# Second token step of a 2-D Fourier filter and its inverse with real and imaginary parts on the partitions, and the middle of the kernel in written order

## The chip, the cores and the metric

The kernel runs on one core of one Trainium2 chip. The metric is the device time of one execution in microseconds (us), as the median of several runs. The engines are named as in the profile: PE (TensorE, with PEld for its weight loads), DVE (VectorE), ACT (ScalarE), POOL (GpSimd) and SP (SyncE, whose queue issues almost all DMAs).

## The reference

Two branches over the same input `x` (1 x 2048 x 1024) are mixed by a gate that is one number per token. Branch A filters `x` by a real two-dimensional Fourier transform, a complex product with a weight W of 2048 x 513, and the inverse. Branch B is a diagonal state-space model of 1024 complex states that runs over the 2048 tokens.

```
g = sigmoid(sum(x * gate_w, -1))
a = irfft2(rfft2(x) * (w_r + 1j*w_i))                      # branch A
h[t] = Lam_bar * h[t-1] + x[t] @ B_bar.T                    # branch B
b = 2 * real(h @ C.T) + x * Dskip
out = g * a + (1 - g) * b
```

All tensors are bf16 in and out.

## The kernel before

**Branch B** works in 16 *units*: 8 chunks `c` of 256 tokens, each in two halves `q` of the states. In `unit` (L203), PE makes the real and then the imaginary part in 32 products of 256 columns each (`psu`, L209; the two parts are called the two halves of a unit here), ACT copies each to a buffer `h` (L211), and DVE does the rest: two products and joins that turn the phases back, two scans (L223), a small carry to the next chunk, and the products and joins that turn them on. 6 buffers `h` stand in turn. From a chunk's two units come two *tiles* of 128 tokens: `c_gemm` (L456) makes `ps_y` in two halves of 16 products of 512 columns and 4 of 128 (Dskip).

**Branch A** is one generator, `gfnet` (L239). 2048 tokens are split as 128 x 16, so that the transform over tokens takes two steps with a turn through DRAM between them. *Step one* (16 times): `fd` transforms over the 1024 features (`ps_fd`, 8 products), and `ps_s1` over 128 tokens with tables T3 (4 products); the result A1 goes to `turn1_scratch`. *Step two* (`s2w`, 16 times): `Bb` comes back with 128 rows that hold 16 blocks of 8; real and imaginary part stand side by side in the free dimension, so `ps_s2` takes 4 products of 512 columns (L354 to L357), the complex product with W 4 instructions of DVE (L361 to L365). The *first inverse step*, `ps_is1` (L375 to L378), takes 4 products with T3, ACT evicts it to C1 and copies a corrected column (L381), and C1 goes to `turn2_scratch`. The *second inverse step* (L387 on) loads it as `Cq` (in the buffer `raw`) and makes `ps_is2` in 8 products of 256 columns; ACT writes ZT. The inverse over the features is `spectral` (`ps_id`, L485), 8 products for each tile.

Column 0 and column 512 are packed into one complex column. `fixup` (L283) unpacks them: the column goes through DRAM (`Acol`, `Bcol`), PE and DVE do a short chain of small steps up to `Qb`, and 64 one-column products (`cps`) make the corrected column of C1.

**Tiles.** 4 *early* tiles are multiplied out before ZT exists and wait in DRAM as `y_scratch` (fp32, eviction `ye`); 4 `late_tile` calls at the end add them. The other 12 are `own_tile`: the spectral part goes into the same PSUM tile by a product with `ident`.

**Order.** The code is traced in one order and a scheduler then sorts each engine's instructions by priority and readiness of their operands; `pull(budget)` (L434) says how much of `gfnet` is traced between two units, by credits such as the 1.73 of `yield 1.73`. PSUM has two pools of two tiles each: `psA` (branch A and own tiles) and `psU` (units, early tiles, `spectral`). Every wait of an engine holds what stands behind it.

Of the kernel before, what the change touches and what calls it, by code (L numbers as in the profile page):

```python
# [19 lines left out]
S = 2048  # L20
D = 1024
# [5 lines left out]
NEARLY = 4  # L27
# [8 lines left out]
def _host_consts():  # L36
# [12 lines left out]
    for cls in range(2):  # L49
# [18 lines left out]
    Kc, Ks = delta * np.cos(angK), delta * np.sin(angK)  # L68
    J = np.zeros((P, P))
# [9 lines left out]
        R12=b16(np.stack([np.concatenate([Kc, Ks], 1), np.concatenate([-Ks, Kc], 1)], 1)),  # L79
# [5 lines left out]
def kernel(  # L85
# [26 lines left out]
    cR12 = nc.inline_tensor(hc["R12"], name="c_R12").ap()  # L112
    cJP = nc.inline_tensor(hc["JP"], name="c_JP").ap()
    Wr_v = A_w_r.rearrange("(p b) k -> p b k", b=16)
    Wi_v = A_w_i.rearrange("(p b) k -> p b k", b=16)
# [85 lines left out]

    def unit(c, q):
        sh = [P, 2, 4, TC]  # L203
        u = halloc(sh, BF16)
        for ri in range(2):
            psu = psU.tile([P, 4, TC], FP32, name="psu", tag="psu")
            for j in range(4):
                for d8 in range(8):
                    nc.tensor.matmul(psu[:, j, :], lhsT=BT[4 * q + j][:, ri, d8, :],  # L209
                                     rhs=xT[:, d8, TC * c:TC * (c + 1)], start=(d8 == 0), stop=(d8 == 7))  # L210
            nc.scalar.copy(out=u[:, ri], in_=psu)  # L211
        js = slice(4 * q, 4 * q + 4)
        bc = lambda i: tab[:, i:i + 1, js, :].to_broadcast(sh)
        su = up.tile(sh, BF16, name="su")
        nc.vector.tensor_mul(out=su, in0=u[:, ::-1], in1=bc(1))  # L215
        nc.vector.tensor_mul(out=u, in0=u, in1=bc(0))  # L216
        nc.vector.tensor_add(out=u[:, 0], in0=u[:, 0], in1=su[:, 0])
        nc.vector.tensor_sub(out=u[:, 1], in0=su[:, 1], in1=u[:, 1])
        if c:
            nc.vector.tensor_add(out=u[:, :, :, 0], in0=u[:, :, :, 0], in1=carry[:, :, js])  # L220
        for ri in range(2):
            seg = u[:, ri].rearrange("p j t -> p (j t)")
            nc.vector.tensor_tensor_scan(out=seg, data0=rz[:, js].rearrange("p j t -> p (j t)"), data1=seg,  # L223
                                         initial=0.0, op0=ALU.mult, op1=ALU.add)
        if c + 1 < NCH:
            gl = u[:, :, :, TC - 1]
            nc.vector.tensor_mul(out=ck[:, 0, :, js], in0=gl, in1=cTC[:, js].unsqueeze(1).to_broadcast([P, 2, 4]))
            nc.vector.tensor_mul(out=ck[:, 1, :, js], in0=gl[:, ::-1], in1=sTC2[:, :, js])
            nc.vector.tensor_add(out=carry[:, :, js], in0=ck[:, 0, :, js], in1=ck[:, 1, :, js])
        sg = up.tile(sh, BF16, name="sg", tag="su")  # L230
        nc.vector.tensor_mul(out=sg, in0=u[:, ::-1], in1=bc(3))  # L231
        nc.vector.tensor_mul(out=u, in0=u, in1=bc(2))  # L232
        nc.vector.tensor_add(out=u[:, 0], in0=u[:, 0], in1=sg[:, 0])
        nc.vector.tensor_sub(out=u[:, 1], in0=u[:, 1], in1=sg[:, 1])
        hs[c, q] = u
# [4 lines left out]
    def gfnet():  # L240
        T3_sb, R12_sb, G_sb = fft["T3"], fft["R12"], fft["G"]
# [14 lines left out]
        for j in range(16):  # L256
# [14 lines left out]
            yield 2.6  # L271
# [6 lines left out]
        gt, wp, JP_sb = fft["gt"], fft["wp"], fft["JP"]  # L278
        Kc_sb, Ks_sb, Kns_sb = fft["K3"][:, 0], fft["K3"][:, 1], fft["K3"][:, 2]
        Wc = fft["Wc"]  # L280

        def fixup():
            zps = psA.tile([P, 2, 16], FP32, name="zps", tag="ps")  # L283
            nc.tensor.matmul(zps[:, 0, :], lhsT=Kc_sb, rhs=Bcol[:, :, 0], start=True, stop=False)
            nc.tensor.matmul(zps[:, 0, :], lhsT=Ks_sb, rhs=Bcol[:, :, 1], start=False, stop=True)
            nc.tensor.matmul(zps[:, 1, :], lhsT=Kc_sb, rhs=Bcol[:, :, 1], start=True, stop=False)
            nc.tensor.matmul(zps[:, 1, :], lhsT=Kns_sb, rhs=Bcol[:, :, 0], start=False, stop=True)
            Zp = fx.tile([P, 16, 2], BF16, name="Zp")
            nc.vector.tensor_copy(out=Zp, in_=zps.rearrange("p c b -> p b c"))
            Zp_f = fx.tile([P, 16, 2], FP32, name="Zp_f"); nc.vector.tensor_copy(out=Zp_f, in_=Zp)  # L290

            def reverse_m(src_bf, ncol, name):
                rps = psA.tile([P, 16, ncol], FP32, name=name + "_ps", tag="ps")
                for b in range(16):
                    if b == 0:
                        nc.tensor.matmul(rps[:, 0, :], lhsT=JP_sb[:, 1, :], rhs=src_bf[:, 0, :], start=True, stop=True)
                    else:
                        nc.tensor.matmul(rps[:, b, :], lhsT=JP_sb[:, 0, :], rhs=src_bf[:, 16 - b, :], start=True, stop=True)
                dst = fx.tile([P, 16, ncol], FP32, name=name)
                nc.vector.tensor_copy(out=dst, in_=rps)  # L300
                return dst

            Wc_f = fx.tile([P, 16, 4], FP32, name="Wc_f"); nc.vector.tensor_copy(out=Wc_f, in_=Wc)
            Wrev = reverse_m(Wc, 4, "Wrev")
            Wh = fx.tile([P, 16, 4], FP32, name="Wh")
            nc.vector.tensor_add(out=Wh[:, :, 0:4:2], in0=Wc_f[:, :, 0:4:2], in1=Wrev[:, :, 0:4:2])
            nc.vector.tensor_sub(out=Wh[:, :, 1:4:2], in0=Wc_f[:, :, 1:4:2], in1=Wrev[:, :, 1:4:2])
            alpha = fx.tile([P, 16, 2], FP32, name="alpha")
            nc.vector.tensor_add(out=alpha, in0=Wh[:, :, 0:2], in1=Wh[:, :, 2:4])
            nc.vector.tensor_scalar_mul(out=alpha, in0=alpha, scalar1=0.25)  # L310
            beta = fx.tile([P, 16, 2], FP32, name="beta")
            nc.vector.tensor_sub(out=beta, in0=Wh[:, :, 0:2], in1=Wh[:, :, 2:4])
            nc.vector.tensor_scalar_mul(out=beta, in0=beta, scalar1=0.25)
            Zr = reverse_m(Zp, 2, "Zrev")
            Q = fx.tile([P, 16, 2], FP32, name="Q")
            q1 = fx.tile([P, 16], FP32, name="q1")
            q2 = fx.tile([P, 16], FP32, name="q2")
            a_re, a_im, b_re, b_im = alpha[:, :, 0], alpha[:, :, 1], beta[:, :, 0], beta[:, :, 1]
            z_re, z_im, zr_re, zr_im = Zp_f[:, :, 0], Zp_f[:, :, 1], Zr[:, :, 0], Zr[:, :, 1]
            nc.vector.tensor_mul(out=q1, in0=a_re, in1=z_re)  # L320
# [26 lines left out]
        def s2w(b):  # L347
# [18 lines left out]
            return X3  # L366

        X3s = [s2w(0), s2w(1)]
        Ccol = fixup()
        for b in range(16):  # L370
            X3 = X3s.pop(0)
            if b + 2 < 16:
# [344 lines left out]
```

## Time and profile before

| | us |
|---|---|
| median of three runs | 396.24 (394.67 to 396.53) |
| the profiled execution | 396.38 |
| its span, first to last instruction | 394.6 |
| PE busy, by the page | 363.6 |
| DVE busy | 294.2 |
| ACT busy | 183.0 |

The span is what the trace shows, and 1.8 us of the execution lie around it. The busy time of PE is modelled (matmuls overlap), so it says where PE had something under way, not how much it got done. In three stretches the kernel reads as follows: up to 98 us `x` is loaded and turned, and step one runs; from 98 to 203 us come the column correction, step two, both inverse steps and parts of seven units and two tiles; from 203 us on, the remaining units, tiles and `spectral`.

### The profile page before, as it was taken

The page shows a single profiled execution, that of the slowest core. Times are in us where ns is not written, and L with a number is a line of the kernel's source. Part 1 is how long each engine was busy: PE and PEld are TensorE (multiplying, and loading weights), DVE is VectorE, ACT ScalarE, POOL GpSimd, SP SyncE. Part 2 cuts the span into 40 slices and gives each one's busy share as a digit, 9 for nine tenths or more (in the row PEclk, how much of TensorE's full clock was granted, in tenths as well). Part 3 has the DMA queues.
Part 4 walks back from the last instruction along what each step waited for, and adds up shares of the span by engine and source line. Part 5 has one row for each costly group of instructions (what it writes and reads, how often), then busy time and mean ns, then how long its engine had stood idle before and what let it go on. Part 6 is the DMA issues. An engine that isn't in the chain of part 4 may idle for free.

```text
span 394.6 us, 6556 instructions
## 1 busy us (share of the span) xinstructions
PE 363.6 (92%) x2625; PEld 239.6 (61%) x2625; DVE 294.2 (75%) x467; ACT 183.0 (46%) x234; POOL 28.8 (7%) x68
## 2 busy tenths in 40 slices
PE   4959998999899799898999999999999999999995
PEld 3836555557665444446777577586685775755552
DVE  2793679186989989896029789889898898897343
ACT  2649898664331288684962232142232231424331
POOL 6600000252300000000000000000000000000000
PEclk9979999999989789999999999999999999999999
DMA  7999921798580269857931010000000000001443
GB/s 205 345 179 241 191 110 55 186 202 184 141 236 8 86 197 318 278 191 193 269 98 55 1 55 28 0 28 27 2 28 0 29 27 2 27 28 27 135 130 110
DMA packets 58078, 45.85 MB, mean 116 GB/s; under 512 B 38720, under 2 KB 43200, under 8 KB 57792
## 3 DMA queue, kind: packets, MB, share of 16 engines
q1 hardware_dynamic: 57616, 45.41, 41.7%
q0 software_dynamic: 352, 0.02, 0.7%
q8 instruction: 20, 0.33, 0.3%
q14 instruction: 10, 0.08, 0.1%
q10 hardware_dynamic: 80, 0.01, 0.0%
HBM read 22.35 MB, written 14.69 MB: 94 GB/s over the span
## 4 chain that ended last, share of the span: by engine, by line
PE 61%; DVE 13%; DMA 11%; ACT 7%; SPq 3%; issue 3%; POOLq 1%; POOL 0%; ACTq 0%; DVEq 0%
PE ps_y L462 23%; PE psu L209 21%; PE ps_fd L249 5%; ACT X L252 3%; DMA Bb<-turn_scratch 3%; DMA raw<-turn_scratch 3%; DMA BT<-in_A_x_dram 3%; PE ps_id L485 3%; DVE h L223 2%; PE ps_y L466 2%; PE ps_is L392 1%; PE ps_y L469 1%; DMA W_b<-in_A_w_i_dram 1%; PE ps_is L394 1%; DMA BT<-in_B_B_re_dram 1%
## 5 line engine op out<-in xcount | busy, mean ns | idle before, releaser
L209 PE MATMUL psu<-xT,BT 128*128 128x256 bf16 x1024 | 123.1, 276 | 1.0 <-DMA BT<-in_B_B_re_dram 0.9
L462 PE MATMUL ps_y<-CT,h 128*128 128x512 bf16 x512 | 116.9, 379 | 0.0
L209 PEld LDWEIGHTS <-BT 128*128 128x128 bf16 x1024 | 100.7, 99 | 20.9 <-issue 1.6
L462 PEld LDWEIGHTS <-h 128*128 128x128 bf16 x512 | 49.9, 98 | 54.6 <-issue 0.4
L223 DVE TENSOR_TENSOR_SCAN h<-rz,h 128x1024 bf16<-128x1024 f32 x32 | 71.8, 2278 | 0.3
L211 ACT CAST h<-psu 128x1024 bf16<-128x1024 f32 x32 | 32.4, 1011 | 58.0 <-PE psu L209 58.0
L215 DVE TENSOR_TENSOR su<-h,tab 128x2048 bf16<-128x2048 bf16 x16 | 19.6, 1225 | 48.4 <-ACT h L211 48.2
L509 ACT ACTIVATE raw<-ps_y,omg 128x512 bf16<-128x512 f32 x24 | 15.2, 683 | 67.9 <-PE ps_y L469 67.9
L249 PE MATMUL ps_fd<-G_sb,preT 128*128 128x512 bf16 x128 | 31.1, 388 | 4.7 <-ACT X L252 4.3
L249 PEld LDWEIGHTS <-preT 128*128 128x128 bf16 x128 | 18.5, 145 | 14.4 <-issue 7.2
L252 ACT CAST X<-ps_fd 128x1024 bf16<-128x1024 f32 x16 | 20.7, 1304 | 7.9 <-PE ps_fd L249 7.9
L359 ACT CAST X<-ps_s 128x1024 bf16<-128x1024 f32 x16 | 16.2, 1013 | 17.1 <-PE ps_s L357 17.1
L216 DVE TENSOR_TENSOR h<-h,tab 128x2048 bf16<-128x2048 bf16 x16 | 19.6, 1223 | 1.3 <-DVE su L215 0.5
L232 DVE TENSOR_TENSOR h<-h,tab 128x2048 bf16<-128x2048 bf16 x16 | 19.6, 1223 | 0.1
L231 DVE TENSOR_TENSOR sg<-h,tab 128x2048 bf16<-128x2048 bf16 x16 | 19.5, 1218 | 0.1
L516 PE MATMUL pt<-ident,BT 128*128 128x128 bf16 x128 | 13.0, 276 | 5.9 <-DMA BT<-in_A_x_dram 5.9
L380 ACT CAST C<-ps_is 128x1024 bf16<-128x1024 f32 x16 | 16.2, 1014 | 3.5 <-PE ps_is L378 3.1
L396 ACT CAST ZT<-ps_is 128x1024 bf16<-128x1024 f32 x16 | 16.1, 1012 | 3.4 <-PE ps_is L394 2.7
L488 ACT ACTIVATE raw<-ps_id,grat 128x1024 bf16<-128x1024 f32 x12 | 13.4, 1113 | 7.8 <-DMA out_dram<-raw 7.8
L392 PE MATMUL ps_is<-R_sb,raw 128*128 128x256 bf16 x64 | 14.9, 273 | 2.1 <-DMA raw<-turn_scratch 2.0
L485 PE MATMUL ps_id<-raw,ZT 128*128 128x256 bf16 x128 | 16.1, 272 | 0.2 <-ACT raw L488 0.2
L267 POOL COPY Acol<-A 128x2 bf16<-128x2 bf16 x16 | 9.9, 619 | 68.6 <-DVE A L266 35.7
(193 smaller groups left out, 459.5 us busy)
## 6 DMA issues: line engine op xcount, KB each, us to landing
BT<-in_A_x_dram SPq DMA_DIRECT2D x8, 512.0 KB, 6.5
turn_scratch<-A SPq DMA_DIRECT2D x16, 256.0 KB, 2.5
Bb<-turn_scratch SPq DMA_DIRECT2D x16, 256.0 KB, 3.8
turn_scratch<-C SPq DMA_DIRECT2D x16, 256.0 KB, 3.3
raw<-turn_scratch SPq DMA_DIRECT2D x16, 256.0 KB, 5.4
out_dram<-raw SPq DMA_DIRECT2D x12, 256.0 KB, 2.1
W_b<-in_A_w_r_dram SPq DMA_DIRECT2D x16, 128.0 KB, 3.9
W_b<-in_A_w_i_dram SPq DMA_DIRECT2D x16, 128.0 KB, 3.8
```

The source lines that it names most:

```text
L209: nc.tensor.matmul(psu[:, j, :], lhsT=BT[4 * q + j][:, ri, d8, :], rhs=xT[:, d8, TC * c:TC * (c + 1)], start=(d8 == 0), stop=(d8 == 7))
L211: nc.scalar.copy(out=u[:, ri], in_=psu)
L215: nc.vector.tensor_mul(out=su, in0=u[:, ::-1], in1=bc(1))
L216: nc.vector.tensor_mul(out=u, in0=u, in1=bc(0))
L223: nc.vector.tensor_tensor_scan(out=seg, data0=rz[:, js].rearrange("p j t -> p (j t)"), data1=seg, initial=0.0, op0=ALU.mult, op1=ALU.add)
L231: nc.vector.tensor_mul(out=sg, in0=u[:, ::-1], in1=bc(3))
L232: nc.vector.tensor_mul(out=u, in0=u, in1=bc(2))
L249: nc.tensor.matmul(ps[:, cls, :], lhsT=preT_A[:, cls, d4, j, :], rhs=G_sb[:, cls, d4, :], start=(d4 == 0), stop=(d4 == 3))
L252: nc.scalar.copy(out=X1.rearrange("p r (i c) -> p c r i", c=2), in_=ps.rearrange("p c (r i) -> p c r i", r=2))
L392: nc.tensor.matmul(psz[:, kc, :], lhsT=Cq[:, 0, P * kc:P * (kc + 1)], rhs=R12_sb[:, 0, :], start=True, stop=False)
L462: nc.tensor.matmul(psy[:, 512 * dh:512 * (dh + 1)], lhsT=hs[c, jb // 4][:, ri, jb % 4, P * tq:P * (tq + 1)], rhs=CT[ri][:, jb, 512 * dh:51 ...
L485: nc.tensor.matmul(pse[:, slot, :], lhsT=ZT_t[:, i, tb, :], rhs=fft["Gi"][:, i, :], start=(kb == 0), stop=(kb == 1))
```

## The change

*Layouts.* In `turn1_scratch` real and imaginary rows of A1 now lie apart, so that a load `Bb` has on its 128 partitions 16 values x (real, imaginary) x 4 blocks, and holds two of 32 blocks side by side. Step two is then one product of 512 columns with a real matrix K2 for each block (2 per pass, 16 passes). W is loaded to both halves of the partitions (four transfers of 64 partitions for each pass, `Wb`, columns 1 to 511; column 0 of `Wb` stays at 1 and 0). DVE makes `X2*Wr` and `X2*Wi` (`V2`), and the first inverse step takes the two as two products with tables MT, where the complex rule is in the tables. `turn2_scratch` is then read in 8 loads of two transfers of 64 partitions, and the second inverse step makes one product of 128 columns with R2 for each of 4 blocks, written to every fourth column of `ps_is2`.

*The column* is now put into X2, ahead of W: `Qb` goes through four small products (`qps`) to `Qn`, which ACT copies into each X2. `cps` is gone.

*Tiles.* 7 early and 7 late tiles, 9 own ones. An own tile is evicted in one piece.

*Order.* From the end of step one on, PE, DVE and ACT keep the order in which the code is written (`manual_schedule`). `unit`, `early` and `own_tile` are generators of halves; DVE's part of a unit is a list of pieces with costs, and `vector(us)` writes that many microseconds of them at each place. SP and POOL are still sorted by the scheduler.

The diff, cut to its core:

```diff
-NEARLY = 4
+NEARLY = 7
...
-    turn1_dram = dram.tile([16, P, 2, K], BF16, name="turn1_scratch")
-    turn2_dram = dram.tile([16, P, 2, K], BF16, name="turn2_scratch")
+    turn1_dram = dram.tile([16, 2, P, K], BF16, name="turn1_scratch")
+    turn2_dram = dram.tile([32, P, K], BF16, name="turn2_scratch")
...
-            nc.sync.dma_start(out=turn1_dram[j], in_=A1)
-            if 7 <= j < 15:
-                load_C(j - 7, A1)
+            nc.sync.dma_start(out=turn1_dram[j].rearrange("r m k -> m r k"), in_=A1)
+            if 6 <= j < 14:
+                load_C(j - 6)
...
+        MT_sb = raw.rearrange("p (b n) -> p b n", n=192)
+        nc.sync.dma_start(out=MT_sb, in_=cMT)
...
+        def load(g):
+            bs = slice(2 * g, 2 * g + 2)
+            Bb = gt.tile([P, 2, K], BF16, name="Bb", tag="gin", bufs=3)
+            nc.sync.dma_start(out=Bb, in_=t1_v[:, bs])
+            for w in range(2):
+                for r in range(2):
+                    nc.sync.dma_start(out=Wb[g % 3][64 * r:64 * (r + 1), w, :, 1:K], in_=W_v[w][:, bs, 1:K])
+            return Bb
...
+        def s2(g):
+            ps2 = psA.tile([P, 2, K], FP32, name="ps_s2", tag="ps")
+            for h in range(2):
+                nc.tensor.matmul(ps2[:, h, :], lhsT=KRS_sb[:, 0, :], rhs=loads[g][:, h, :], start=True, stop=True)
+            X2 = gt.tile([P, 2, K], BF16, name="X2", tag="gev", bufs=4)
+            nc.scalar.copy(out=X2, in_=ps2)
+            nc.scalar.copy(out=X2[:, :, 0], in_=Qn[:, 2 * g:2 * g + 2])
+            return X2
+
+        def times_w(g, X2):
+            V2 = gt.tile([P, 2, K], BF16, name="V2", tag="gv2", bufs=2)
+            nc.vector.tensor_mul(out=V2, in0=X2, in1=Wb[g % 3][:, 1])
+            nc.vector.tensor_mul(out=X2, in0=X2, in1=Wb[g % 3][:, 0])
+            return X2, V2
...
+        for g in range(16):
+            if g + 2 < 16:
+                X2s.append(s2(g + 2))
             psc = psA.tile([P, 2, K], FP32, name="ps_is1", tag="ps")
+            for h in range(2):
+                b = 2 * g + h
+                nc.tensor.matmul(psc[:, h, :], lhsT=MT_sb[:, b, 64:192], rhs=UV[0][:, h, :], start=True, stop=False)
+                nc.tensor.matmul(psc[:, h, :], lhsT=MT_sb[:, b, 0:128], rhs=UV[1][:, h, :], start=False, stop=True)
...
+            nc.sync.dma_start(out=turn2_dram[2 * g:2 * g + 2].rearrange("b m k -> m b k"), in_=C1)
+            yield "is1"
+            if g + 1 < 16:
+                UV = times_w(g + 1, X2s.pop(0))
+            if g + 3 < 16:
+                loads.append(load(g + 3))
+            yield "uv"
...
+        for G in range(8):
+            Cq = raw[:, 2 * D * (G % 3):2 * D * (G % 3 + 1)].rearrange("p (g k) -> p g k", g=4)
+            for r in range(2):
+                nc.sync.dma_start(out=Cq[64 * r:64 * (r + 1)], in_=t2_v[G, r])
+            for kp in range(2):
+                psz = psA.tile([P, 2, K], FP32, name="ps_is2", tag="ps")
+                for kl in range(2):
...
+                    for g in range(4):
+                        nc.tensor.matmul(pv[:, :, g::4], lhsT=Cq[:, g, P * kc:P * (kc + 1)], rhs=KRS_sb[:, 1, :],
+                                         start=True, stop=True)
...
+    ssm = chain(unit(0, 0), unit(0, 1), unit(1, 0), unit(1, 1),
+                early(0), unit(2, 0), early(1), unit(2, 1), early(2), unit(3, 0), early(3), unit(3, 1),
+                early(4), unit(4, 0), early(5), unit(4, 1),
+                early(6), unit(5, 0))
+    for j in range(5, 16):
+        step()
+        if j % 3:
+            halves(ssm, 1)
+        vector(3.5)
+    guard = tc.manual_schedule(engines={mybir.EngineType.PE, mybir.EngineType.DVE, mybir.EngineType.Activation})
+    guard.__enter__()
+    for v, n in (("w", 3), ("z", 2), ("q", 2), ("qn", 1), ("s2", 0), ("uv", 1)):
+        assert step() == v
+        for _ in range(n):
+            halves(ssm, 1)
+            vector(3.0)
+    for g in range(16):
+        assert step() == "is1"
+        assert step() == "uv"
+        halves(ssm, 1)
+        vector(3.3)
...
+    for g in range(16):
+        assert step() == "is2"
+        if g == 0:
+            after_ic()
+        if g % 2:
+            halves(ssm, 1)
+        vector(2.0)
```

How the order of three places changes. The names are those of the trace's program: `DVE_49` and the like are semaphores, `DMAHW0` to `DMAHW7` eight semaphores that the transfers take in turn, `raw` holds T3 before and MT now at these places.

PE where the corrected column is made; before:

```order
L209 MATMUL psu<-xT,BT_117 128x256
L337 LDWEIGHTS raw
L337 MATMUL cps<-Qb,raw 128x1 [waits DVE_49]
L338 LDWEIGHTS raw
L338 MATMUL cps<-Qb,raw 128x1
L339 LDWEIGHTS raw
L339 MATMUL cps<-Qb,raw 128x1
L340 LDWEIGHTS raw
L340 MATMUL cps<-Qb,raw 128x1
```

and now, where `ps_y` is tile 1:

```order
L537 LDWEIGHTS xT
L537 MATMUL ps_y<-dgD,xT 128x128
L416 LDWEIGHTS Sel_sb [waits DMAHW5_49]
L416 MATMUL qps<-Qb,Sel_sb 128x16 [waits DVE_49]
L416 LDWEIGHTS Sel_sb
L416 MATMUL qps<-Qb,Sel_sb 128x16
```

Before, `cps` stands behind 22 unit products that follow tile 1, and 60 more `cps` products follow it; now `qps` stands right behind tile 1. Between `zps` (the column's first products) and `qps` there are now 64 unit products, the reversal and tile 1; before, there were 50 and 22 unit products, both reversals, and tile 0.

PE in step two and the first inverse step; before, one of 16 passes:

```order
L209 MATMUL psu<-xT,BT_117 128x256
L354 LDWEIGHTS K_sb [waits DMAHW6_49]
L354 MATMUL ps_s_1615<-Bb,K_sb 128x512 [waits Activation_49]
L355 LDWEIGHTS K_sb
L355 MATMUL ps_s_1615<-Bb,K_sb 128x512
L356 LDWEIGHTS K_sb
L356 MATMUL ps_s_1615<-Bb,K_sb 128x512
L357 LDWEIGHTS K_sb
L357 MATMUL ps_s_1615<-Bb,K_sb 128x512
L375 LDWEIGHTS raw
L375 MATMUL ps_is_1628<-X_1348,raw 128x512 [waits Activation_49]
```

and now:

```order
L537 MATMUL ps_y<-dgD,xT 128x128
L425 LDWEIGHTS KRS_sb [waits DMAHW3_49]
L425 MATMUL ps_s_1862<-Bb,KRS_sb 128x512 [waits Activation_49]
L425 LDWEIGHTS KRS_sb
L425 MATMUL ps_s_1862<-Bb,KRS_sb 128x512
L449 LDWEIGHTS raw [waits DVE_49]
L449 MATMUL ps_is_1868<-X_1761,raw 128x512 [waits Activation_49]
L450 LDWEIGHTS raw
L450 MATMUL ps_is_1868<-V_1822,raw 128x512
```

Before, some two unit products stand between two groups of 4; now a whole half of a unit (32 products) or of a tile (20) stands ahead of 2 products of step two (two passes ahead) and 4 of the inverse.

SP at the same place; before, one pass and the start of the next:

```order
L349 DMA Bb<-turn_scratch 128x1024 [waits DMAHW4_49,PE_49]
L382 DMA turn_scratch<-C_1687 128x1024 [waits DMAHW5_49,Activation_49]
L351 DMA W_b<-in_A_w_r_dram 128x512 [waits DMAHW6_49,DVE_49]
L352 DMA W_b<-in_A_w_i_dram 128x512 [waits DMAHW7_49]
L349 DMA Bb<-turn_scratch 128x1024 [waits DMAHW0_49,PE_49]
L382 DMA turn_scratch<-C_1714 128x1024 [waits DMAHW1_49,Activation_49]
```

and now:

```order
L351 DMA Bb<-turn_scratch 128x1024 [waits DMAHW3_49,PE_49]
L354 DMA Wb_1333<-in_A_w_r_dram 64x2x511 [waits DMAHW4_49,DVE_49]
L354 DMA Wb_1333<-in_A_w_r_dram 64x2x511 [waits DMAHW5_49]
L453 DMA turn_scratch<-C_1935 128x2x512 [waits DMAHW6_49,Activation_49]
L354 DMA Wb_1333<-in_A_w_i_dram 64x2x511 [waits DMAHW7_49]
L354 DMA Wb_1333<-in_A_w_i_dram 64x2x511 [waits DMAHW0_49]
L351 DMA Bb<-turn_scratch 128x1024 [waits DMAHW1_49,PE_49]
```

Now the four W transfers of a pass stand around the store of C1 of four passes earlier, and the next `Bb` behind them.

More of the change, by code (lines that the diff above doesn't have):

```diff
@@ L200, in halloc @@
         return pool.tile(shape, dtype, name="h")
+    work = []
     def unit(c, q):
@@ L211, in unit, with vector, vector_until @@
             nc.scalar.copy(out=u[:, ri], in_=psu)
[L212 to L235, printed above, removed]
+            if ri == 1:
+                work.extend([(2.4, turn_back), (1.5, join), (2.3, lambda: scan(0)), (2.3, lambda: scan(1)),
+                             (0.5, carry_on), (2.4, turn), (1.4, join_on)])
+            yield 3.5
+    owed = [0.0]
+    def vector(us):
+        owed[0] += us
+        while work and owed[0] > 0:
+            cost, piece = work.pop(0)
+            piece()
+            owed[0] -= cost
+        if not work:
+            owed[0] = min(owed[0], 0.0)
+    def vector_until(c):
+        while (c, 0) not in hs or (c, 1) not in hs:
+            cost, piece = work.pop(0)
+            piece()
+            owed[0] -= cost
     fft = {}
     def gfnet():
-        T3_sb, R12_sb, G_sb = fft["T3"], fft["R12"], fft["G"]
+        T3_sb, G_sb = fft["T3"], fft["G"]
         Acol = fx.tile([P, 16, 2], BF16, name="Acol")
@@ L384, in gfnet @@
[L384 to L398 removed]
+        KRS_sb = fft["KRS"]
```

418 lines of the change are left out of this document (223 added, 195 removed).

## The prediction

> **What bounds the kernel now.** I read the page first, then the busy time by stretches, then the chain and the groups of the slow stretch. Columns of the stretches: length, busy time and instructions of each engine, granted TensorE clock, DMA share, GB/s.
>
> ```profile
> PE 363.6 (92%) x2625; PEld 239.6 (61%) x2625; DVE 294.2 (75%) x467; ACT 183.0 (46%) x234; POOL 28.8 (7%) x68
> 110.00:141.00 31.00, 28.02 (x248) 17.85 (x247) 28.58 (x60) 8.04 (x10) 0.00 (x0) 0.84 0.33 108
> 141.00:181.00 40.00, 38.37 (x203) 18.69 (x202) 37.43 (x68) 31.89 (x47) 0.00 (x0) 1.00 0.74 245
> 181.00:203.00 22.00, 19.95 (x170) 15.86 (x168) 3.10 (x5) 16.76 (x17) 0.00 (x0) 1.00 0.91 237
> 203.00:358.00 155.00, 154.43 (x1109) 104.86 (x1108) 135.62 (x170) 41.73 (x50) 0.00 (x0) 1.00 0.06 21
> ```
>
> TensorE is the bound, but a busy PE in the middle is not PE at its pace: 203 matmuls in 40 us there against 1109 in 155 us behind it. The true pace comes from unbroken pieces of the chain (start, us, what):
>
> ```profile
> 211.31 6.99 PE psu L209 x64
> 218.30 3.45 PE ps_y L462 x16
> 207.41 0.22 PE ps_y L466 x4
> 257.20 0.87 PE ps_id L485 x8
> 133.26 0.16 PE cps L337
> 135.10 0.45 PE ps_s L354
> ```
>
> So a 256-column product costs 0.109 us, a 512-column one 0.216, a 128-column one with its own weight load 0.055; the 64 one-column `cps` products take 1.84 us (133.26 to 135.10). What PE had to do between 98 (end of token step one) and 203 (end of the inverse's second step), by line (busy, mean ns, idle ahead):
>
> ```profile
> L209 PE MATMUL psu<-xT,BT 128*128 128x256 bf16 x249 | 33.4, 280 | 0.0
> L462 PE MATMUL ps_y<-CT,h 128*128 128x512 bf16 x64 | 15.3, 379 | 0.0
> L392 PE MATMUL ps_is<-R_sb,raw 128*128 128x256 bf16 x64 | 14.9, 273 | 2.1 <-DMA raw<-turn_scratch 2.0
> L356 PE MATMUL ps_s<-Bb,K_sb 128*128 128x512 bf16 x16 | 6.8, 426 | 0.0
> L378 PE MATMUL ps_is<-X,raw 128*128 128x512 bf16 x16 | 6.3, 394 | 0.0
> L337 PE MATMUL cps<-Qb,raw 128*128 128x1 bf16 x16 | 1.8, 165 | 2.9 <-DVE Qb L334 2.9
> ```
>
> At the pace above: 249 x 0.109 = 27.2; 64 x 0.216 with 16 small ones = 14.7; the second inverse step has two such lines, 128 x 0.109 = 14.0; step two and the first inverse step four lines each, 128 x 0.216 = 27.6; `cps` and the other column products 2.8; a rest of step one 1.1. Sum 87.4 of 105 us: **17.6 us are lost there**, to the wait for `Qb`, to the clock of 0.84 in 110-141 and to transfers. Behind 203 almost nothing is lost (154.43 of 155).
>
> **The change, part by part.** *Products removed.* Step two: 32 products of 512 columns instead of 64, -6.9 us. Second inverse step: 128 of 128 columns instead of 128 of 256, -7.0 (0.055 is the `L466` row; the new ones write every fourth column, which no row shows: between 0.055 and 0.109, so 0 to 7 us more; I take 0.055, since that row has the same columns and weight load). `ident` products of three tiles, 6 x 0.216, -1.3. `cps` gives way to four 16-column products, -1.7. In all -16.9. *Moved:* nine more halves of units and three more tiles go from the dense end into the middle. In its place I build the new run by stages.
>
> *Up to the end of step one.* The order on PE is the old one but for 28 unit products that now stand ahead of the last step-one product: 98 + 28 x 0.109 = 101. The column corrections (GpSimd copies ahead of the C loads) are gone and 16 stores become 1 KB rows instead of 2 KB; both lie beside PE work: 0 (-1 to +2).
>
> *The middle.* By the order PE has there 482 unit products (52.6 us), 7 early tiles of 7.34 (32 x 0.216 + 8 x 0.055; 51.4), step two 6.9, first inverse step 13.8, second 7.0, small ones 1.1: 132.8 us. What can be lost, place by place:
>
> (a) The columns' way through DRAM. Before:
>
> ```profile
> 98.49 1.02 ACT A L266
> 100.75 1.25 SPq L453 DMA_TRANSPOSE CT<-in_B_C_re_dram  x1
> 102.09 1.25 SPq L453 DMA_TRANSPOSE CT<-in_B_C_im_dram  x1
> 106.43 0.65 SPq L276
> 112.15 3.05 DMA Bb<-turn_scratch
> Bcol<-col_scratch SPq DMA_DIRECT2D x1, 8.0 KB, 3.8
> 10.00:20.00 10.00, 9.21 (x154) 8.78 (x155) 7.23 (x24) 6.76 (x11) 6.31 (x21) 1.00 1.04 346
> ```
>
> `Bcol` was issued at 106.43 and landed 3.8 later or at 110.9 with the issue's own time, 12.4 us behind the eviction's start. The two C loads that held SP from 100.75 to 103.4 now go earlier; 1.5 MB of `MT` goes ahead instead, 4.5 us at the 346 GB/s of the last row: 9.7 to 14.3. PE has 11.2 us in between (half a unit, the reversal, tile 0). Loss 0 to 3, I take 2. Behind that each vector step of the columns has 7 us of PE work beside it in the new order (64 unit products, then tile 1), where 2.9 were idle and the clock fell: 0.
>
> (b) The loop of 16 passes. One pass: step two 0.43, inverse 0.86, half a unit or tile 3.5 or 3.67: 4.87 us. Its other engines:
>
> ```profile
> L359 ACT CAST X<-ps_s 128x1024 bf16<-128x1024 f32 x16 | 16.2, 1013 | 17.1 <-PE ps_s L357 17.1
> L380 ACT CAST C<-ps_is 128x1024 bf16<-128x1024 f32 x16 | 16.2, 1014 | 3.5 <-PE ps_is L378 3.1
> L381 ACT COPY C<-Ccol 128x2 bf16<-128x2 bf16 x16 | 3.3, 204 | 0.3
> L476 ACT ACTIVATE ye<-ps_y,omg 128x512 f32<-128x512 f32 x8 | 5.1, 683 | 20.5 <-PE ps_y L466 20.5
> L396 ACT CAST ZT<-ps_is 128x1024 bf16<-128x1024 f32 x16 | 16.1, 1012 | 3.4 <-PE ps_is L394 2.7
> L361 DVE TENSOR_TENSOR X<-X,W_b 128x1024 bf16<-128x1024 bf16 x16 | 11.0, 686 | 3.9 <-ACT X L359 3.4 <-DMA W_b<-in_A_w_r_dram 0.3
> 344.37 1.24 DVE su L215
> 356.16 0.60 DVE h L234
> ```
>
> ScalarE: two evictions of 1.01, a column of 0.2, one unit eviction of 1.01: 3.3. VectorE: two products of 0.69 (the two 512-wide adds go) and a quarter of a unit, which runs from 344.37 to 356.76, 12.4 us: 1.4 + 3.1 = 4.5. Both fit into 4.87. `s2(g+2)` stands two passes ahead of its use, so its eviction (1.0) and both products (1.4) have a pass to spare. Transfers: per pass `Bb` 256 KB, W 512 KB (both halves of the partitions get the same rows, twice the old bytes), `C1` 256 KB, and two `ye` in four: some 1.05 to 1.18 MB, or 16.9 MB over 78 us, 217 GB/s, below the 245 that the stretch 141-181 ran at a share of 0.74. SP:
>
> ```profile
> L351 SPq DMA_DIRECT2D W_b<-in_A_w_r_dram x16: 328/382/1598, 107.1 to 168.1; - x16
> DMA to landing us min/median/max: 2.2/3.8/4.6
> ```
>
> 6.5 issues of 0.4 are 2.6 us of a pass. The W rows wait on SP for VectorE's products of three passes before, and behind them on SP stand the `C1` store and the next `Bb`; that wait is done two passes ahead, so nobody is late. Loss 0 to 0.4 a pass; I take 2 us for the loop.
>
> (c) The second inverse step: PE 7.0 and one unit 7.0, but ScalarE 16 x 1.01 + 2 x 1.01 + tile 6 at 2 x 0.68: 19.5, and about 5.2 MB, 20 to 22 us at 237 to 257 GB/s, that start 5 us before PE gets there (the last store is covered by half a unit and tile 6, 11 us). ScalarE decides: 21 us with the first latency, 7 lost. Here the old cover (35 + 15 unit products) is thinner, not gone.
>
> A rule speaks against (c): the Trainium skill, "SBUF — State Buffer", section "Door 1: The DMA port swizzle", measures 196 GB/s for a transfer to 64 partitions against 328 for 128, and says that two transfers to the two halves hardly add up. All W loads and the new loads of this step are of 64 partitions; by it (an estimate) these 4.2 MB take 21.4 us and the sum below would be 373; no run here shows a transfer of 64 partitions.
>
> *The end.* 5 units 35.0, 9 own tiles of 7.77 (70.0), 16 x 0.87 = 13.9: 118.9, dense as before if VectorE follows.
>
> ```profile
> 385.11 0.42 DVE L490 TENSOR_TENSOR raw<-raw 128x512 bf16<-128x512 bf16 x1
> 385.45 0.42 DVE L491 TENSOR_TENSOR raw<-raw 128x512 bf16<-128x512 bf16 x1
> L502 DVE TENSOR_TENSOR ga<-yl,ga 128x512 bf16<-128x512 f32 x8 | 5.5, 689 | 9.3 <-DMA yl<-y_scratch 9.3
> 390.09 0.69 ACT raw L509
> L488 ACT ACTIVATE raw<-ps_id,grat 128x1024 bf16<-128x1024 f32 x12 | 13.4, 1113 | 7.8 <-DMA out_dram<-raw 7.8
> ```
>
> A step with a unit and a late tile (three of them) asks of VectorE 12.4, two late adds of 0.69 and 8 short adds 0.34 apart: 16.5, of PE 16.5 too; the steps behind have 9.5 us of PE for 4 of VectorE, and the last unit is used three steps after it is made, so a lag of 2 or 3 us is taken up: 0 (to +3). The last eviction comes in one piece, 1.11 instead of 0.69: +0.4 on the 4.6 us behind PE's last product.
>
> **Sum:** 101 + 132.8 + (2 + 2 + 7) + 118.9 + 5.0 = 368.7 us of span, and 1.8 around it (396.38 - 394.6): 370.5. The profiled run's 396.38 is as good as the median, 396.24. Against before: -16.9 of products, -6.6 of lost time (17.6 to 11), +0.4, and some -2.5 that 203 to 390 held beyond its products and that rounding of counts makes. I say **370 us**.
>
> **Rivals.** *The middle loses as much as before* (17.6 instead of 11): the written order lets PE run nothing out of turn, where the old one slipped two unit products into each gap. For it: PE has no other work at hand now when a wait comes. Against: each wait in (b) has a pass of margin. Time 377 (375 to 383).
> *W paces the loop*: twice the 1 KB packets, landing at an odd byte offset. 346 GB/s on 16 engines is 95 ns of one for a 2 KB packet; the stretch 141-181 (245 at 0.74, a third of it in 1 KB packets) then gives some 52 ns for those. A pass has 192 of the one and 768 of the other: 58 us of an engine, 3.6 us of all. Should the 512 of W cost double, 5.3: 16 x 0.43 = 7 more, 378; triple, 404. Against: the old W rows were as long, and odd at their source.
> *Slower than before*: the loop is set by landings. SP lets eight transfers be under way (each row waits for the one eight before it), and a pass has 6.5. At a landing of 3.8 that allows a pass in 3.1 us; it decides from 6 us, and from 8 us a pass takes 6.5, +26 us: 396. At 9 us: 7.3 a pass, 409. Against: the longest landing seen is 4.6 for W, 6.2 for `raw`; it would have to double.
> *Hardly any loss*: second inverse step and columns covered as well: 361.
>
> **How the numbers follow.** Forecast's own case (364 to 375) 0.57; as much loss 0.20; W paces 0.08; landings 0.06; hardly any loss 0.07; the rest unnamed. The range 362 to 386 leaves out most of landings and half of the last case, and takes in the unknown column stride (+7). Within 0.5% (394.3 to 398.2; less a measurement of this kernel can't tell from no change) only landings near 8 us fall: 0.03. Faster 0.91, slower 0.06.
>
> **What would show it.** Step two with 32 products, the second inverse step with 0.055 between products; the loop's 16 passes 4.9 us apart, PE clock 1.00 from 110 on; idle PE mainly in the second inverse step, put down to ScalarE's `ZT` or `raw`; the end's period 16.5 us, then 9.5. Wrong if `is1` waits for `V` or `Wb`, if landings pass 6 us, or if PE waits for VectorE's `h` at early tiles.

## Result: 372.7 us, and where the time went

The changed kernel takes 372.69 us (median of 4 runs, 371.52 to 373.50), the kernel before 395.46 (4 runs): ratio 0.943, 95% interval 0.9376 to 0.9483, 22.8 us less. The prediction was 370 (362 to 386). The profiled execution took 373.5, its span is 371.7, so 1.8 us lie around it as before. Ratios and their intervals leave out runs in the chip's slower state: none of the changed kernel, and one of the first experiment's four (375.45; the median of its other three is 372.35).

First the busy line of its page and the stretches that answer to those of before (length; busy time and instructions of PE, PEld, DVE, ACT, POOL; granted TensorE clock, DMA share, GB/s). The borders are the stages' own: columns to 138, loop to 215, second inverse step to 247, then the end.

```profile
PE 345.2 (93%) x2499; PEld 236.3 (64%) x2527; DVE 290.2 (78%) x441; ACT 180.4 (49%) x225; POOL 19.3 (5%) x58
101.00:138.00 37.00, 34.80 (x286) 24.57 (x288) 32.69 (x63) 10.67 (x14) 0.53 (x7) 1.00 0.58 161
138.00:215.00 77.00, 76.58 (x501) 48.17 (x507) 74.39 (x94) 43.59 (x60) 0.00 (x0) 1.00 0.76 209
215.00:247.00 32.00, 29.80 (x236) 23.54 (x234) 24.96 (x28) 19.24 (x21) 0.00 (x0) 1.00 0.67 181
247.00:331.00 84.00, 82.82 (x605) 58.01 (x611) 71.23 (x101) 25.24 (x25) 0.00 (x0) 1.00 0.13 39
```

From 101 on the clock is 1.00 everywhere (0.84 in one stretch before). 77 us of loop have 501 products (6.5 a us) where 40 us had 203 (5.1). Now the chain (start, us, what), at the places on which the terms of the sum rested: the end of step one and the columns; four passes of the loop; the second inverse step; one step of the end.

```profile
97.42 3.51 PE psu L273 x32
...
102.91 8.04 DMA turn_scratch<-A
...
115.33 7.00 PE psu L273 x64
...
138.04 0.43 PE ps_s L425 x2
...
143.01 0.43 PE ps_s L425 x2
...
157.56 0.43 PE ps_s L425 x2
...
222.61 1.75 PE ps_is L474 x16
...
247.24 0.83 PE ps_id L562 x6
...
279.36 7.00 PE psu L273 x64
...
287.44 1.03 PE ps_id L562 x8
...
296.26 7.00 PE psu L273 x64
...
367.37 1.11 ACT raw L591
```

Step one ends at 100.93 (97.42 + 3.51), where the prediction had 101. The last store of step one lands 8.04 us after its issue, and the columns come behind it. Four passes take 19.52 us (138.04 to 157.56), 4.88 each. The second inverse step runs from 222.61 to 247.24, 24.6 us, and 16 of its products take 1.75: **0.109 us each, not 0.055**. Steps of the end take 16.9 us (279.36 to 296.26). The products of the stretch 101 to 247, by line (busy, mean ns, idle ahead):

```profile
L273 PE MATMUL psu<-xT,BT 128*128 128x256 bf16 x480 | 54.8, 273 | 0.0
L474 PE MATMUL ps_is<-KRS_sb,raw 128*128 128x128 bf16 x128 | 15.4, 311 | 1.6 <-DMA raw<-turn_scratch 1.2 <-ACT ZT L476 0.5
```

That these 128-column products last 311 ns, longer than the 256-column ones (273), is the first sign of what the experiments show.

By the prediction's own stages: 100.9 + 146.3 (to 247.24) + 120.1 (to the last product's end, 367.34) + 4.3 = 371.7, against 101 + 143.8 + 118.9 + 5.0 = 368.7.

### The profile page after: what moved, and what is told of

Same layout as the page of the kernel before. It is cut to its first block, busy times and chain, and to the rows that moved or that the text cites. A ratio compares the mean times of both kernels' runs of the same rounds, so it can differ in the third digit from the quotient of the medians.

```text
span 371.7 us, 6369 instructions
## 1 busy us (share of the span) xinstructions
PE 345.2 (93%) x2499; PEld 236.3 (64%) x2527; DVE 290.2 (78%) x441; ACT 180.4 (49%) x225; POOL 19.3 (5%) x58
## 4 chain that ended last, share of the span: by engine, by line
PE 73%; ACT 9%; DMA 8%; DVE 7%; issue 2%; SPq 1%; ACTq 0%; DVEq 0%
PE psu L273 26%; PE ps_y L533 26%; PE ps_fd L310 6%; PE ps_id L562 3%; DMA BT<-in_A_x_dram 3%; ACT X L313 3%; DMA turn_scratch<-A 2%; PE ps_is L449 2%; PE ps_is L474 2%; ACT h L275 2%; PE ps_is L450 2%; PE ps_y L537 2%; PE ps_s L425 2%; DMA raw<-turn_scratch 1%; PE ps_y L540 1%
## 5 line engine op out<-in xcount | busy, mean ns | idle before, releaser
L273 PE MATMUL psu<-xT,BT 128*128 128x256 bf16 x1024 | 118.8, 274 | 1.4 <-DMA BT<-in_B_B_re_dram 1.4
L533 PE MATMUL ps_y<-CT,h 128*128 128x512 bf16 x496 | 113.2, 379 | 0.8
L591 ACT ACTIVATE raw<-ps_y,omg 128x1024 bf16<-128x1024 f32 x9 | 10.0, 1113 | 53.3 <-PE ps_y L540 53.3
L310 PE MATMUL ps_fd<-G_sb,preT 128*128 128x512 bf16 x122 | 29.8, 381 | 4.8 <-ACT X L313 3.9
L550 ACT ACTIVATE ye<-ps_y,omg 128x512 f32<-128x512 f32 x14 | 8.9, 683 | 29.1 <-PE ps_y L537 15.9
L599 PE MATMUL pt<-ident,BT 128*128 128x128 bf16 x128 | 14.0, 292 | 4.9 <-DMA BT<-in_A_x_dram 4.9
L569 DVE TENSOR_TENSOR raw<-raw 128x512 bf16<-128x512 bf16 x16 | 6.7, 422 | 15.0 <-DMA out_dram<-raw 12.7
L562 PE MATMUL ps_id<-Gi_sb,ZT 128*128 128x256 bf16 x128 | 16.3, 273 | 1.4 <-ACT ZT L476 0.8
L474 PE MATMUL ps_is<-KRS_sb,raw 128*128 128x128 bf16 x128 | 15.4, 311 | 1.6 <-DMA raw<-turn_scratch 1.2
```

The source lines that it names most:

```text
L310: nc.tensor.matmul(ps[:, cls, :], lhsT=preT_A[:, cls, d4, j, :], rhs=G_sb[:, cls, d4, :], start=(d4 == 0), stop=(d4 == 3))
L474: nc.tensor.matmul(pv[:, :, g::4], lhsT=Cq[:, g, P * kc:P * (kc + 1)], rhs=KRS_sb[:, 1, :], start=True, stop=True)
L533: nc.tensor.matmul(psy[:, 512 * dh:512 * (dh + 1)], lhsT=hs[c, jb // 4][:, ri, jb % 4, P * tq:P * (tq + 1)], rhs=CT[ri][:, jb, 512 * dh:51 ...
L562: nc.tensor.matmul(pse[:, slot, :], lhsT=ZT_t[:, i, tb, :], rhs=fft["Gi"][:, i, :], start=(kb == 0), stop=(kb == 1))
```

## Experiments

Small differences are read from the traces, stage by stage. The median of the kernel before differs by 1.4 us from one set of runs to the next (395.07 to 396.44), and single runs of one kernel differ by more, with the granted clock: the four runs of the second experiment below go from 373.37 at a mean clock of 0.991 to 378.20 at 0.982.

**What does a 128-column product cost, and why?** In the second inverse step each product has its own weights and writes every fourth column. Either could be what doubles it.

```
- pv = psz[:, kl, :].rearrange("p (n t) -> p n t", t=8)
- nc.tensor.matmul(pv[:, :, g::4], lhsT=Cq[...], rhs=KRS_sb[:, 1, :], ...)
+ nc.tensor.matmul(psz[:, kl, P*g:P*(g+1)], lhsT=Cq[...], rhs=KRS_sb[:, 1, :], ...)
  # and the eviction reads psz as "p kl (g n x) -> p kl n x g"
```

> The 128 products of the second inverse step write 128 contiguous columns of PSUM instead of every fourth one; the eviction reads them with the stride instead. Theory 'stride': the products took 0.109 us instead of 0.055 because of the writing stride; now 16 of them take 0.9 us instead of 1.75, PE's share of that stage falls by 7 us, and as ScalarE (16 x 1.0 + 2 x 1.0) and the loads then decide, the stage ends 2 to 4 us earlier: 369 to 371. Rival 'weight load': each of these products has weights of its own, and a weight load takes 0.104 us (16 in 1.66), so the pace stays at 0.105 to 0.109 and the time at 372 to 374, if the eviction keeps its 0.97 us.

The chain of this run:

```profile
114.71 8.57 PE psu L273 x64
...
223.55 0.89 PE ps_is L473 x16
...
233.38 3.67 ACT ZT L475 x4
...
238.29 4.64 DMA raw<-turn_scratch
...
246.10 0.83 PE ps_id L561 x6
```

16 products take 0.89 us, 0.056 each: the stride it was. The stage takes 22.55 us (223.55 to 246.10) instead of 24.63, 2.1 less, with ScalarE evicting four times without a gap (3.67) and the last rows' landing (4.64) on the chain: PE's 7 us come to 2.1, because ScalarE is next and the loads behind it. What TensorE's products of this stage waited for shows it (total, times); in the changed kernel the same two were 0.5 and 1.2:

```profile
L473 PE MATMUL ps_is<-KRS_sb,raw x128: 216/219/312, 223.4 to 244.4; 128*128 128x128 bf16 x128
...
  ACT ZT L475: 3.9, 7
...
  DMA raw<-turn_scratch: 0.4, 1
```

The median, 372.61 (ratio 0.9377, 0.9315 to 0.9439), lies in the rival's range and does not tell this kernel from 372.69. What tells the two theories apart is the pace in the trace, and there the rival's 0.105 to 0.109 did not hold. In the columns of this profiled run 64 products took 8.57 us instead of 7.00, at a granted clock of 0.91 in 101 to 120 against 1.00; that took back 1.6 us.

```
+ for r in range(2):
+     nc.tensor.matmul(pv[:, 32*r:32*(r+1), g::4], lhsT=Cq[...], rhs=KRS_sb[:, 1, 64*r:64*(r+1)], ...)
```

> Each product of the second inverse step is made as two of 64 columns (256 products instead of 128), with the same weights loaded for each; columns and stride as before in sum. Theory 'weight load': one product takes as long as its weight load, about 0.105 us whatever its columns, so 16 more products a block of 16: PE has 256 x 0.105 = 27 us instead of 14, the stage grows by 11 to 13.5 us: 384 to 386. Rival 'stride' (time goes by columns written): 0.055 each, PE's sum unchanged, 372 to 374.

```profile
100.76 3.51 PE psu L273 x32
...
225.89 1.79 PE ps_is L475 x32
...
251.53 0.83 PE ps_id L563 x6
```

32 products of 64 strided columns in 1.79 us: 0.056 each, with a weight load for every one. So the weight load is not what sets 0.109; the time goes by columns, and a strided one costs twice a contiguous one (0.109/128 against 0.056/128). The stage takes 25.6 us, 1.0 more. The median, 376.30, is far from the 384 to 386 of the weight load, and above the other theory's 372 to 374. In the profiled run (377.78) 3.3 us come from ahead of the changed place: step one's last unit products start at 100.76 instead of 97.42, and 32 unit products near 36 us took 6.30 us instead of 3.67, with a granted clock of 0.80 in 25 to 50 against 0.93. The Trainium skill, "SBUF — State Buffer", section "Door 1: The DMA port swizzle", says that any non-contiguous access pattern in PSUM significantly slows matmuls; the runs agree for this pattern, every fourth column, and give its size: twice.

**Does TensorE pace the loop?** Every product of step two made three times.

```
+ for _ in range(3):
      nc.tensor.matmul(ps2[:, h, :], lhsT=KRS_sb[:, 0, :], rhs=loads[g][:, h, :], start=True, stop=True)
```

> Every product of step two is made three times (96 of 512 columns instead of 32), nothing else. Theory: TensorE paces the loop at 4.88 us, so 4 x 0.216 = 0.86 us more a pass, 5.74 a pass, +13.8 us in all: 386.5. Rival (the loop is paced by transfers or by the way over ScalarE and VectorE, TensorE has room): 4.9 to 5.2 a pass, +0 to +5: 373 to 378.

```profile
100.55 3.51 PE psu L273 x32
...
148.85 1.29 PE ps_s L426 x6
...
154.68 1.29 PE ps_s L426 x6
```

A pass with a tile takes 5.83 us (148.85 to 154.68) where it took 4.97 (138.04 to 143.01): exactly the 0.86 us of products added. The median is 389.17, 16.5 more. The profiled span is 16.9 longer: 3.1 lie ahead of the loop, where the granted clock was 0.80 in 25 to 50 again, and 13.8 in it. TensorE paces the loop.

**How much room is beside it?** The loop without the half unit or tile between its products.

```
      assert step() == "uv"
+     vector(3.3)
+ for _ in range(16):
      halves(ssm, 1)
      vector(3.3)
```

> The 16 passes of the loop are written without the half unit or tile that each had between its products; these 16 pieces follow behind the loop, ahead of the second inverse step. It shows the loop's own floor. A pass has 1.29 us of products. Theory 'margin': the floor is the transfers, 1.05 MB a pass at up to 346 GB/s, or ScalarE's 2.2 us with its waits: 3.0 to 4.0 us a pass, so 27 to 43 us more: 400 to 416. Rival 'the loop stood at its limit already' (landings or rows of W near 4.9): 4.6 us or more a pass, +53 or more: 426 and above.

428.41 us (ratio 1.081, 1.0753 to 1.0867): the rival's number. The waits in 145 to 200 (total, times, longest):

```profile
PE ps_s L425 <- DMA Bb<-turn_scratch: 29.4, 10, 5.7
DVE V L433 <- DMA Wb<-in_A_w_i_dram: 25.3, 7, 5.8
```

The first inverse step's products by their line (min/median/max ns, first and last start), two a pass:

```profile
L449 PE MATMUL ps_is<-X,raw x32: 376/634/634, 139.7 to 211.9; 128*128 128x512 bf16 x32
```

W's way from issue to landing, and the stretch 145 to 205:

```profile
DMA to landing us min/median/max: 2.9/3.7/4.6
```

```profile
145.00:205.00 60.00, 27.69 (x68) 7.59 (x69) 31.16 (x43) 24.32 (x34) 0.00 (x0) 0.65 0.76 197
```

The passes take 4.8 us on average (71.4 us in 15 steps, the last product being the second of its pass, 0.8 behind the first) with 1.3 us of products in them at full clock: this loop waits for landings, and some of that goes back to SP's order: W's issue stands behind an earlier pass's `C1` store, for which SP stood idle from 157.59 to 159.88, for example. It is not the floor of the loop in the changed kernel, though, where nobody waits for W or `Bb` and e3's products came through in full: here the granted clock fell to 0.65 and a 512-column product lasted 634 ns instead of 379. How far below 4.88 the other engines could go at full clock stays open. The prediction's 3.1 us a pass for the queue was too low in any case, since SP's issues alone take 3.5 us in the changed kernel (4 of 0.60 for W, 0.55 for `Bb`, 0.54 for `C1`). Half of W's bytes, in the bare loop (this kernel leaves half of W out of the computation):

```
- out=Wb[g % 3][64*r:64*(r+1), w, :, 1:K], in_=W_v[w][:, bs, 1:K]
+ out=Wb[g % 3][64*r:64*(r+1), w, :, 1:H], in_=W_v[w][:, bs, 1:H]
```

> The bare loop with only the first 255 columns of each W row loaded (the other columns keep the constant they are preset with): half of W's bytes, the same number of issues and packets. It leaves half of W out of the computation. Theory 'bytes': the loop's own floor is set by what the transfers move (1.05 MB a pass at about 195 GB/s is 5.4 us); with 0.79 MB it is 4.1 us, 16 x 1.3 = 21 us less: 405 to 410. Rival 'issue and latency': six issues of 0.6 us on SP and the way landing, products, eviction, store set it, whatever the bytes: 423 to 429.

The same landing and stretch in this run:

```profile
DMA to landing us min/median/max: 2.4/2.6/3.4
```

```profile
145.00:205.00 60.00, 27.81 (x74) 7.90 (x76) 29.40 (x40) 25.59 (x35) 0.00 (x0) 0.73 0.56 152
```

422.62 us, 5.8 less, just below the rival's 423 to 429: a quarter of a pass's bytes gone, the share of the DMA engines down from 0.76 to 0.56, and a pass only some 0.3 us shorter. Bytes are not what binds the bare loop, or a pass would have lost 1.3 us. What is left is the way through issue, landing (1.1 us shorter), product, eviction and store; that is argued, as no run takes it apart, and the granted clock differed too (0.73 against 0.65).

The same transfers cut so that each reaches 128 partitions:

```
- out=Wb[g % 3][64*r:64*(r+1), w, :, 1:K], in_=W_v[w][:, bs, 1:K]          # r = 0, 1
+ out=Wb[g % 3][:, w, h, 1:K], in_=AP([[0, 2], [32*(K+1), 64], [1, K-1]])  # h = 0, 1
```

> The bare loop (no unit or tile between its products, 428.4 us) with the same four W transfers a pass cut the other way: each fills all 128 partitions with one row b (its 64 source rows read twice) instead of 64 partitions with two rows b. Same bytes, packets and issues. Theory 'partitions': a transfer to 64 partitions is slower than one to 128, so W lands sooner than 3.7 us after its issue and the passes of 5.4 us become 4 to 4.8: 410 to 420. Rival 'packets and issues': landing stays near 3.7 us and the time at 425 to 431.

The share of the DMA engines in tenths and the GB/s, 150 to 200 in 40 slices; then the issues of W on SP (min/median/max ns):

```profile
DMA  0997001111351111111465161111119921111111
GB/s 0 344 247 254 13 29 34 47 49 46 70 210 49 47 49 62 47 49 47 171 152 189 69 212 48 48 48 48 47 49 277 324 92 47 51 49 47 49 47 48
```

```profile
L355 SPq DMA_DIRECT2D Wb<-in_A_w_r_dram x32: 511/2390/3470, 111.1 to 298.2; - x32
```

535.02 us, which neither theory had. For long stretches a tenth of the DMA engines is busy and 47 to 49 GB/s flow, which fits two engines of sixteen (two sixteenths of the 346 GB/s of the prediction's row are 43); an issue takes 2.39 us on SP instead of 0.61. The source's outermost dimension is now the repeat of two. The Trainium skill, "DMA: Bandwidth & Descriptors", section "Rules for kernel authors", says that a leading zero-stride broadcast of c copies confines a transfer to c engines at most; the trace agrees (47 to 49 GB/s), though no run changes the order of the dimensions alone. So this run says nothing on 64 against 128 partitions, and that question stays open.

**Columns.** MT's 1.5 MB from ScalarE's queue, behind the matmuls of `zps`.

```
- nc.sync.dma_start(out=MT_sb, in_=cMT)        # in step "w"
+ nc.scalar.dma_start(out=MT_sb, in_=cMT)      # behind zps, in step "z"
```

> As after, but the 1.5 MB of MT are issued from ScalarE's queue behind the matmuls of zps, so that the last store of step one and the two transfers of the columns go ahead of them. Theory: in after that store landed 8.04 us after its issue (2.57 before the change) and the columns behind it, so zps waited 2.0 us on TensorE; now zps starts 12 us instead of 14.1 behind the end of step one's unit products, and nothing else waits: 2 us less, 370.5 to 371. Rival 'the wait only moves': W rows and Bb meet MT later, step two or the first inverse step waits for them: 372 to 374.

The wait of the changed kernel that this aims at (total, times, longest):

```profile
PE zps L382 <- DMA Bcol<-col_scratch: 2.0, 1, 2.0
```

Two rows of the chain of this run:

```profile
96.69 3.49 PE psu L273 x32
...
112.38 7.00 PE psu L273 x64
```

From the end of step one's unit products to the 64 products behind `zps`: 12.2 us (100.18 to 112.38) instead of 14.4 (100.93 to 115.33), and the wait is gone from the list. 370.57 us (ratio 0.9371, 0.9340 to 0.9403): 2.1 less, as expected.

**The written order.** Without it, TensorE's rows hardly differ up to the end; VectorE's and ScalarE's do.

```
- guard = tc.manual_schedule(engines={mybir.EngineType.PE, ...})
- guard.__enter__()
```

> As after, without the written order: TensorE, VectorE and ScalarE are sorted by the scheduler, as they were before the change. TensorE's rows stay as they are up to the end of the second inverse step, VectorE's and ScalarE's differ. Theory: with PE at 4.88 us a pass and 3 to 8 us between a W row's landing and its use, a vector step earlier or later is taken up; 371 to 374. Rival 'the written order carries the gain' (one late product of VectorE stops TensorE, as the 17.6 us lost before the change): 378 to 384.

376.63 us (ratio 0.952, 0.9484 to 0.9557), 3.9 more: between both theories. The stretch of the columns, a wait, and a piece of the chain:

```profile
101.00:138.00 37.00, 32.41 (x243) 21.61 (x242) 34.57 (x67) 7.10 (x9) 2.62 (x7) 0.92 0.53 147
```

```profile
PE qps L416 <- DVE Qb L411: 2.5, 1, 2.5
```

```profile
115.05 8.56 PE psu L273 x64
...
144.39 0.38 PE ps_is L449
...
149.09 0.43 PE ps_s L425 x2
...
154.06 0.43 PE ps_s L425 x2
```

It lies in the columns: the first inverse product starts near 144.4, where in the changed kernel it follows the step two of 138.04, some 6 us; PE waits 2.5 us for `Qb` (2.9 before the change), and the clock is 0.92. Of the 6 us, 1.6 are the 64 products of 8.56 instead of 7.00; they come ahead of that wait, and e1 had the same 8.57 in written order, so this part is not the order's. From there on a pass has its 4.97 (149.09 to 154.06), and the later stages give back 1.4 (the span is 4.7 longer). So the written order is worth 3 to 4 us in all, at one place; the loop doesn't need it.

**The end and the cover.** `ps_id` of the next tile behind the present tile's first half:

```
+ for hf, _ in enumerate(own_tile(tb, ga)):
+     if hf == 0 and tb + 1 < 16:
+         ga_next = spectral(tb + 1, grat)
```

> As after, but the ps_id products of the next own tile are written behind the first half of the present one instead of ahead of it. Theory: three steps of the end run 16.9 us instead of 16.5, because these products wait 0.4 us for ScalarE's eviction of the unit just made, out of the same two buffers; now the buffer is long free: 16.5 a step, 1.2 us less, 371.5. Rival 'VectorE sets these steps' (16.5 us of work in each): the wait moves to the own tile's product with ga and the steps stay at 16.9: 372.7.

```profile
277.90 6.99 PE psu L273 x64
...
294.41 6.99 PE psu L273 x64
```

16.51 us a step instead of 16.90: the 0.4 was the wait for ScalarE's eviction out of the same two buffers. 371.88 us; the 1.2 us of three such steps are in the trace, the median (370.52 to 375.68) is too coarse for them.

Unit (5,1) moved into the second inverse step, alone and with contiguous writes:

```
- early(6), unit(5, 0))
+ early(6), unit(5, 0), unit(5, 1))
- units = [(5, 1), (6, 0), (6, 1), (7, 0), (7, 1)]
+ units = [None, (6, 0), (6, 1), (7, 0), (7, 1)]
```

> As after, but unit (5,1) is written into the second inverse step (behind its 4th and 5th group of rows) instead of at the start of the end. Theory 'strided products fill the stage': PE needs 14.0 us for its 128 products there, with 7.0 of a unit and a wait of 2.4 in all; 7.0 us more of unit work can take up 2.4 at the most, so 1.5 to 2.4 us less than after's 372.7: 370 to 371.5. Rival 'the prediction's account' (products of 0.055, ScalarE decides, 7 us lost): 5 to 7 us less: 366 to 368.

> The same move together with contiguous writes in the second inverse step. Theory: the 128 products take 7.1 us there instead of 14, so the two evictions and 7.0 us of a moved unit find room beside ScalarE's 16 x 0.95: the stage stays at 23 to 25 us while the end gives up 7.0: 365.5 to 368, some 5 less than either edit's best alone (370). Rival 'ScalarE or the loads decide the stage and the unit only lengthens it': 370 to 372.

Alone 371.43 (ratio 0.9408, 0.9383 to 0.9433), 1.3 less: there was little idle time to fill. With contiguous writes 368.87 (0.9353, 0.9317 to 0.9388), 3.8 less, short of 365.5 to 368, with a new wait of 1.3 us on TensorE (the run with both edits):

```profile
PE ps_y L539 <- DVE raw L571: 1.3, 1, 1.3
```

In the written order the first own tile's adds stood on VectorE behind all of the moved unit.

**Together**, with those adds ahead of the rest of the unit (`vector(2.0)` for the first 13 of 16 groups only) and the last eviction in halves:

> What helped, together: MT behind zps, contiguous writes in the second inverse step, unit (5,1) moved there, ps_id of the next own tile behind the present one's first half, VectorE's pieces of the moved unit written behind the adds of the first own tile, and the last eviction in two halves. Theory: the gains lie in different stages and add up: 372.7 - 2.1 (columns) - 3.8 (contiguous with the moved unit) - 1.3 (the wait of the first own tile for VectorE in that run) - 1.2 (end) - 0.4 (last eviction) = 363.9, within 362.5 to 365.5. Rival: they don't add, as VectorE, which had 16.5 us of work in each of three steps of 16.5 us, sets the end once TensorE waits nowhere: 366 to 368.

```profile
220.21 0.89 PE ps_is L473 x16
...
246.19 0.83 PE ps_id L561 x6
...
358.17 0.69 ACT raw L591
```

**363.80 us** (363.39 to 364.85; ratio 0.920, 0.9171 to 0.9229), 8.9 less than the changed kernel: the gains lie in different stages and add up. The second inverse step takes 26.0 us (220.21 to 246.19) with 7.0 us of unit more in it, and the wait for VectorE's adds is gone from the list.

## Why the prediction was right, and where its sum was off

*Up to the end of step one*, 101: 100.93.

*Products removed.* Step two at half its products and the tiles without `ident` came as counted. The step that failed is "second inverse step, -7.0 (0.055)": its stride was called unknown, with "0 to 7 us more", and all 7 came (14.0 instead of 7.0; e1, e2). So the change removed some 10 us of products, not 16.9.

*(a) Columns*, 2 of 0 to 3: 2.0 of waiting, for the reason given, MT ahead on the queue (e9).

*(b) Loop*, 4.87 a pass and 2 lost: 4.88 and nothing lost; TensorE paces it (e3). The ease claimed beside it was less than said: issues of W on SP (min/median/max ns) took 0.60 us, not 0.4, W's landings came near the 6 us that the prediction named as a sign against it, and an emptied loop waits for landings (e4).

```profile
L354 SPq DMA_DIRECT2D Wb<-in_A_w_r_dram x32: 595/601/1531, 112.2 to 192.8; - x32
DMA to landing us min/median/max: 2.9/4.0/5.7
```

The rivals on W and on landings did not occur: in the changed kernel nobody waits for W or `Bb`. As far as the trace tells landings, the 6 us were passed outside the loop only, by the last store of step one (8.04) and by a load `raw` (7.1).

*(c) Second inverse step*, 7.0 of products, 7.0 of unit, 7 lost, 21 in all: 14.0, 7.0 and 3.6, 24.6 in all. The two errors offset each other by half: products of twice the length fill the time that would have been lost to ScalarE. With contiguous writes, the case that the prediction described, it is 22.55, and ScalarE decides, as it said (3.9 us of TensorE's waits against 0.4 for `raw`, e1). The prediction took ScalarE's 21 us as the length whatever the products cost, and counted 7 us more for strided ones on top in its range. Neither is so: 7 us of products move the stage by 2.1, and without them it still takes 1.6 more than 21.

*The end*, 118.9 (0 to +3): 120.1. The 1.2 is three waits of `ps_id` for ScalarE (e10), not VectorE. Its period is 16.9 us instead of 16.5, and behind the last unit 9.5 as said. *Behind the last product*, 5.0: 4.3.

Sum of the differences: +3.6 for (c), -2 for (b), +1.2 (end), -0.7 (last eviction); with +0.9 spread over the rest of the middle, 3.0. Lost time in the middle is 6.5 us (146.3 less 139.8 of products) against 17.6 before and 11 forecast. So 11 of the 22.8 us gained are lost time that went, 3 to 4 of them by the written order (e11), and some 10 are products. That 370 came within 2.7 us of 372.7 is in part luck: 7 us of products were missing from the sum, and half of them were offset by time that it had put down as lost. *The middle loses as much as before* did not hold; nor did *hardly any loss*, whose 361 needed the products of 0.055. The 372.7 lies near the 373 by the rule on 64 partitions, but the trace does not bear that out as the mechanism: TensorE waited 1.2 us for `raw` in the second inverse step and 0.4 with contiguous writes, and what the sum lacked is accounted for without it, but for the 0.9. What 64 partitions cost a transfer stays open (e5).

## To carry to other kernels

Price a product by what it reads and also by how it writes: a row with the same columns but another pattern in PSUM is no price for it, and one run with a contiguous write settles it. When a stage has two engines near its length (here TensorE's strided products and ScalarE's evictions), halving the one gives only the gap to the other, until work from a dense stage is moved into the room. On a queue that the scheduler sorts (SP's here), a big load that is free to go early stands ahead of a small transfer that somebody waits for. In a written order, moved vector work stands ahead of adds that the next tile needs. Both are found by reading each queue for what stands before the thing waited for.

## What was not expected of the hardware

A 128-column product that writes every fourth column of PSUM takes 0.109 us, a contiguous one 0.056, a strided one of 64 columns 0.056, each with its own weights: the stride doubles the time, and a weight load for each product does not show in it. A 256 KB store queued behind a 1.5 MB load landed 8.04 us after its issue, where the kernel before had 2.57; with the load moved (e9), the transfer that waits for this store was issued 2.3 us behind it (102.17 and 104.46). In the emptied loop the granted clock fell to 0.65, and a 512-column product lasted 634 ns instead of 379. A transfer whose source begins with a repeat of two moved 47 to 49 GB/s, and took SP 2.39 us to issue.
